# A carried state's products as four 64x64 products in the four quarters of TensorE

## The chip, the cores and the metric

The kernel runs on one core of one Trainium2 chip. The metric is the device time of one execution in microseconds; the time before is the median of three runs. All data is fp32.

## The reference, cut to what matters

A state-space layer (Mamba2 SSD) is followed by a sum of four gated two-layer networks. The layer works through a sequence in chunks. In each chunk it adds what the tokens of the chunk give one another (`y_intra`) to what the state carried over from earlier chunks gives (`y_inter`), and then renews the state:

```python
batch, n_heads, seq, head_dim, d_state = (4, 8, 768, 32, 16)
...
y_intra = np.einsum('bhij,bhjd->bhid', M, xc)
decay_to_i = np.exp(cum)
y_inter = np.einsum('bhin,bhnd->bhid', Cc, state) * decay_to_i[:, :, :, None]
y[:, :, sl] = y_intra + y_inter
...
state = decay_full[:, :, None, None] * state + np.sum(Bx, axis=2)
...
# second block: x is y with heads and head_dim joined, (3072, 256); E = 4, F = 1024
for e in range(E):
    h = np.maximum(x @ w1[e], 0.0)
    out += p[:, e:e + 1] * (h @ w2[e])
```

The change concerns `y_inter`, the product of `Cc` (16 state entries for each of 8 heads) with the state.

## The kernel before

The kernel cuts each of the 4 sequences into 6 chunks of 128 tokens: 24 chunks. Four chunks, one of each sequence, form a block of 512 tokens (`CPB = 4`, `NBLK = 6`); chunk `c` belongs to block `k = c // 4` and to sequence `i = c % 4`. The first block has no state yet, so 20 chunks have a product with it. The networks' products are done by Strassen's scheme (seven products of halves in place of eight) and fill most of TensorE's time; `fmul` is the first layer, `smul` the second.

The 8 heads lie as 4 groups `q` of 32 partitions, each with two heads `t`. A state product works on all 128 partitions: `lhsT` is `M`, the state, spread so that only the four 32x32 blocks on the diagonal are not zero, and `rhs` is `cts`, 2 x 128 = 256 columns.

```python
def load_tokens(c):
    xb = load.tile([P, W], FP32, tag="xb", name="xb", bufs=4)
    nc.sync.dma_start(out=xb, in_=xbc[real(c)])
    ...
def load_heads(c):
    ah = st[c]["ah"] = load.tile([HN, P], FP32, tag="ah", name="ah", bufs=4)
    nc.sync.dma_start(out=ah, in_=ac_d[real(c)].unsqueeze(1).to_broadcast([NH, N, P]))
...
# decay_part(c, 2): the decay of the state to each token, on the rows of C
    nc.vector.tensor_tensor_scan(out=dec, data0=s["ah"], data1=zeros, initial=1.0, ...)
    nc.gpsimd.tensor_mul(cts, s["ctm"], dec.unsqueeze(1).to_broadcast([HN, NT, P]))
...
def scores(cs, homes):                      # C times B, four row tiles of 32
    ...
    for j, c in enumerate(cs):
        for q in range(NQ):
            k = slice(32 * q, 32 * q + 32)
            nc.tensor.matmul(                                          # line 376
                out=s["g"][q]..., lhsT=s["xb"][k, OBT:OBT + P], rhs=s["ctm"][k]...,
                start=(j == 0), stop=True, tile_position=(32 * q, 0), ...)
...
def outputs(cs):                            # cs: two chunks
    for c in cs:
        ys[c] = y = ps_att.tile([P, NT, P + N], FP32, tag="att", name="y")
        if k > 0:
            nc.tensor.matmul(                                          # line 398
                out=y[:, :, 0:P], lhsT=state[i][1].rearrange("p q d -> p (q d)"),
                rhs=st[c]["cts"], start=True, stop=False, skip_group_check=True)
    for c in cs:
        for t in range(NT):
            for q in range(NQ):
                nc.tensor.matmul(                                      # line 408
                    out=y[32 * q:32 * q + 32, t, 0:w], lhsT=s["xb"][:, h * D:h * D + D],
                    rhs=s["MT"][:, NT * q + t, 0:w], tile_position=(0, 32 * q), ...)
    for c in cs:
        nc.scalar.copy(out=yT[k][:, :, i * P:i * P + P], in_=y[:, :, 0:P])   # line 417
        if k < NBLK - 1:
            s["A"] = att.tile([P, NT, N], FP32, tag="A", name="A", bufs=4)
            nc.scalar.copy(out=s["A"], in_=y[:, :, P:])                # line 420

def carry(c):                               # the new state S, and M for the next chunk
    nc.vector.transpose(S, s["A"]...)
    ...
    nc.vector.tensor_mul(M, S.unsqueeze(1).to_broadcast([HN, NQ, D]), qmask)
    state[c % CPB] = S, M
```

In the main loop, a step `n` is one part of the weights of a network (two steps for each network and block). Twice in a block of eight steps, two chunks of the next block are prepared: `scores` and `masked` at the end of one step, `outputs` within the next:

```python
    fmul(n, 6); snap(n, 6)                  # snap: ScalarE copies the bank X out
    smul(n - 1, 3)
    if done:
        outputs(done)                       # two chunks
        states.extend(done)
    fmul(n, 5); fmul(n, 7); snap(n, 7)
    total(n, 7, "22")                       # VectorE: z = Y + snap
    smul(n - 1, 7); smul(n - 1, 5)
    ...
```

Line 465 is `fmul`, line 550 `smul`, line 472 `snap`, line 477 `total` (tile `z`).

Of the kernel before, what the change touches and what calls it, by code (L numbers as in the profile page):

```python
# [12 lines left out]
P = 128  # L13
NQ, NT = 4, 2
# [3 lines left out]
def kernel(  # L18
# [38 lines left out]
    nc = tc.nc  # L57
# [3 lines left out]
    NH = NQ * NT  # L61
# [3 lines left out]
    CPB = BLK // P  # L65
    NBLK = NCH // CPB
    T = NCH * P
    OB, OBT, OCT = DM, DM + HN, DM + 2 * HN
    N = HN // NH
# [7 lines left out]
    def real(c):  # L77

        return c % CPB * NBLK + c // CPB
# [15 lines left out]
    ac_d = tc.dram_tile([NCH, NH, P], FP32, name="ac_d")  # L95
# [6 lines left out]
    st = {}  # L102
    SPREAD = 3

    def load_tokens(c):
        xb = load.tile([P, W], FP32, tag="xb", name="xb", bufs=4)
        nc.sync.dma_start(out=xb, in_=xbc[real(c)])
        st.setdefault(c, {})["xb"] = xb

    def load_decays(c):  # L110
# [5 lines left out]
    def load_heads(c):  # L116

        ah = st[c]["ah"] = load.tile([HN, P], FP32, tag="ah", name="ah", bufs=4)
        nc.sync.dma_start(out=ah, in_=ac_d[real(c)].unsqueeze(1).to_broadcast([NH, N, P]))

    def load_chunk(c):
        load_tokens(c)
        load_decays(c)
        load_heads(c)
# [66 lines left out]
    for queue, c in ((nc.sync, slice(0, 1)), (nc.scalar, slice(1, SPREAD))):  # L191
        queue.dma_start(
            out=a_q.rearrange("(q r) c t s -> q r c (t s)", q=NQ)[:, 0, c],
            in_=a.rearrange("(i k) (q t) s -> k q i (t s)", k=NBLK, t=NT)[0][:, c])
    warm = const.tile([P, 1], FP32, name="warm")
    nc.scalar.mul(warm, ones[:, 0:1], ones[:, 0:1])
    load_tokens(0)
    nc.sync.dma_start(
        out=a_sb, in_=a.rearrange("c h s -> (c h) s").rearrange("(p r) s -> p r s", r=2))
    load_tokens(1)  # L200
    load_w1(0)
    load_tokens(2)
# [161 lines left out]
    def scores(cs, homes):  # L364

        for c in cs:
            st[c]["g"] = []
        for pool, tag in homes:
            g = pool.tile([P, len(cs), NT, P], FP32, tag=tag, name="g")
            for j, c in enumerate(cs):  # L370
                st[c]["g"].append(g[:, j])
        for j, c in enumerate(cs):
            s = st[c]
            for q in range(NQ):
                k = slice(32 * q, 32 * q + 32)
                nc.tensor.matmul(  # L376
                    out=s["g"][q].rearrange("p t s -> p (t s)"), lhsT=s["xb"][k, OBT:OBT + P],
                    rhs=s["ctm"][k].rearrange("p t s -> p (t s)"),
                    start=(j == 0), stop=True, tile_position=(32 * q, 0),
                    skip_group_check=True)  # L380

    def masked(cs, qs):
        for q in qs:
            h = slice(NT * q, NT * q + NT)
            for c in cs:
                s = st[c]
                nc.vector.tensor_mul(s["MT"][:, h, 0:P], s["g"][q], s["LT"][:, h])  # L387

    state = {}

    def outputs(cs):

        ys = {}
        for c in cs:
            k, i = divmod(c, CPB)
            ys[c] = y = ps_att.tile([P, NT, P + N], FP32, tag="att", name="y")
            if k > 0:
                nc.tensor.matmul(  # L398
                    out=y[:, :, 0:P], lhsT=state[i][1].rearrange("p q d -> p (q d)"),
                    rhs=st[c]["cts"], start=True, stop=False, skip_group_check=True)  # L400
        for c in cs:
            s, y = st[c], ys[c]
            k, i = divmod(c, CPB)
            w = P + N if k < NBLK - 1 else P
            for t in range(NT):
                for q in range(NQ):
                    h = NQ * t + q
                    nc.tensor.matmul(  # L408
                        out=y[32 * q:32 * q + 32, t, 0:w], lhsT=s["xb"][:, h * D:h * D + D],
                        rhs=s["MT"][:, NT * q + t, 0:w], start=(k == 0 and t == 0), stop=True,  # L410
                        tile_position=(0, 32 * q), skip_group_check=True)
        for c in cs:
            s, y = st[c], ys[c]
            k, i = divmod(c, CPB)
            if i == 0:
                yT[k] = ffn.tile([P, NT, BLK], FP32, tag="yT", name="yT")
            nc.scalar.copy(out=yT[k][:, :, i * P:i * P + P], in_=y[:, :, 0:P])
            if k < NBLK - 1:
                s["A"] = att.tile([P, NT, N], FP32, tag="A", name="A", bufs=4)
                nc.scalar.copy(out=s["A"], in_=y[:, :, P:])  # L420

    def carry(c):
        s = st.pop(c)
# [234 lines left out]
    homes = ((ps_s, "acc0"), (ps_s, "acc1"), (ps_att, "att"), (ps_att, "att"))  # L658
# [12 lines left out]
    turn(1, 3)  # L671
    masks(0)
    scores([0], homes)
    decays(0)
    masks(1)
    spread(1)
    store_decays()
    masks(2)
    masked([0], range(NQ))
    outputs([0])  # L680
    scores([1], banks)
    decays(1)
    turn_gates(ps_att, "att")
    spread(2, (0,))
    spread_gate(ps_att, "att")
    masked([1], range(NQ))
    outputs([1])
    spread(2, (1,))
    sum_w1(0, 0)
# [5 lines left out]
    decays(2)  # L695
    plain_first(0, 1, (0,))
    scores([2], homes)
    plain_first(0, 1, (1,))
    masks(3)
# [4 lines left out]
    load_w2(3)  # L704
    gated(0, "11", "X")
    masked([2], range(NQ))
    outputs([2])

    scores([3], ((ps_s, "acc0"), (ps_s, "acc1"), (ps_s, "acc2"), (ps_att, "att")))
# [36 lines left out]
    for n in range(PLAIN, NS):  # L746
        k, r = divmod(n, SPB)
# [63 lines left out]
        for c in done:  # L811
            if c + CPB < NCH:
                load_tokens(c + CPB)
                load_heads(c + CPB)
# [74 lines left out]
```

## Time and profile before

| | |
|---|---|
| time, median of 3 runs | 646.47 us (646.44 to 647.34) |
| span of the profiled run | 643.5 us |
| TensorE busy | 636.3 us (99%) |
| VectorE busy | 483.9 us (75%) |
| ScalarE busy | 115.5 us (18%) |
| GpSimd busy | 108.3 us (17%) |
| granted TensorE clock | 0.998 of full speed |
| state products (line 398) | 40 records for 20 chunks, first at 69.4 us, last at 525.8 us |

PE is TensorE's matmul, PEld its loading of weights, DVE VectorE, ACT ScalarE, POOL GpSimd, SP the engine that issues most loads. A line of the groups gives the line of the kernel, the engine, the operation, the tile written and the tiles read, the shape (for a matmul rows * columns of the array, then the output), the count, and after the bar the busy time in all, the mean duration of one in ns and the idle time before them. Matmuls are pipelined, so a duration overlaps the next one; the distance between starts tells what one costs. An fp32 matmul leaves two records.

### The profile page before, as it was taken

What the parts mean: (1) busy time and instruction counts of PE and PEld (TensorE: products, weight loads), DVE (VectorE), ACT (ScalarE), POOL (GpSimd) and SP (SyncE); (2) the same over time, 40 slices, a digit from 0 to 9 for tenths busy, and PEclk for the clock granted to TensorE, in tenths of its full rate; (3) what the DMA queues carried; (4) which work ended last, traced back from release to release, by engine and by line L of the source; (5) the groups of instructions that cost most, each with busy time, mean ns of one, the idle gap of its engine ahead of it and who ended that gap; (6) DMA issues with size and microseconds to landing.
All of it is one profiled execution on the core that took longest, in us unless ns stands there. A gap on an engine that the chain in (4) does not pass through costs nothing.

```text
span 643.5 us, 9107 instructions
## 1 busy us (share of the span) xinstructions
PE 636.3 (99%) x3367; PEld 544.7 (85%) x3367; DVE 483.9 (75%) x809; ACT 115.5 (18%) x247; POOL 108.3 (17%) x157
## 2 busy tenths in 40 slices
PE   8999999999999999999999999999999999999997
PEld 5788878888888888888888888888888888888886
DVE  7869998788777688778688778768877667756555
ACT  3011121212111121112121211122121211111110
POOL 4788565020001002100002000000100000100000
PEclk9999999999999999999999999999999999999999
DMA  7987982855576391668284557548265744256000
GB/s 228 329 293 249 335 324 91 317 182 163 173 210 240 101 356 52 236 182 250 84 294 148 170 185 218 213 147 311 83 214 151 261 152 130 63 169 220 1 0 34
DMA packets 95648, 121.61 MB, mean 189 GB/s; under 512 B 28520, under 2 KB 77556, under 8 KB 95604
## 3 DMA queue, kind: packets, MB, share of 16 engines
q1 hardware_dynamic: 92776, 111.20, 52.8%
q0 software_dynamic: 2304, 9.44, 3.8%
q8 instruction: 27, 0.44, 0.3%
q10 hardware_dynamic: 524, 0.39, 0.2%
q14 instruction: 17, 0.14, 0.1%
HBM read 108.16 MB, written 12.83 MB: 188 GB/s over the span
## 4 chain that ended last, share of the span: by engine, by line
PE 96%; DVE 1%; DMA 1%; SPq 0%; ACT 0%; issue 0%; POOL 0%; ACTq 0%; DVEq 0%; POOLq 0%
PE acc L550 43%; PE X L465 24%; PE Y L465 19%; PE acc L531 2%; PE y L408 2%; PE g L376 2%; PE y L398 1%; PE X L514 1%; PE Y L514 1%; DMA xb<-in_xbc_dram 1%; DVE hT L494 0%; DVE h L487 0%; DVE z L477 0%; DVE LT L348 0%; SPq L134 0%
## 5 line engine op out<-in xcount | busy, mean ns | idle before, releaser
L477 DVE TENSOR_TENSOR z<-Y,snap 128x512 f32<-128x512 f32 x138 | 94.5, 685 | 127.5 <-ACT snap L472 76.4
L550 PE MATMUL acc<-hT,wt 128*128 128x256 f32 x736 | 181.3, 379 | 0.0
L472 ACT COPY snap<-X 128x512 f32<-128x512 f32 x138 | 80.8, 586 | 468.4 <-PE X L465 392.3
L550 PEld LDWEIGHTS acc<-hT,wt 128*128 128x128 f32 x736 | 140.0, 190 | 18.8
L550 PE MATMUL acc<-h,wt 128*128 128x256 f32 x552 | 142.6, 381 | 0.0
L465 PE MATMUL X<-yS,wt 128*128 128x256 f32 x552 | 141.8, 379 | 0.0
L550 PEld LDWEIGHTS acc<-h,wt 128*128 128x128 f32 x552 | 104.2, 190 | 16.9 <-issue 3.0
L465 PEld LDWEIGHTS X<-yS,wt 128*128 128x128 f32 x552 | 105.0, 190 | 14.3 <-issue 0.3
L487 DVE SCALAR_TENSOR_TENSOR h<-z,gate 128x512 f32<-128x512 f32 x138 | 100.1, 725 | 3.5 <-PE acc L531 0.4
L465 PE MATMUL Y<-yT,wt 128*128 128x256 f32 x368 | 94.7, 380 | 1.2 <-DVE z L477 1.2
L465 PEld LDWEIGHTS Y<-yT,wt 128*128 128x128 f32 x368 | 68.8, 190 | 12.3 <-DVE z L477 1.9
L494 DVE TENSOR_TENSOR hT<-h,hT 128x512 f32<-128x512 f32 x92 | 65.2, 709 | 1.8
L494 DVE TENSOR_TENSOR hT<-h,h 128x512 f32<-128x512 f32 x92 | 65.6, 754 | 1.1
L348 DVE TENSOR_TENSOR_SCAN LT<-ab,ident 128x512 f32<-128x512 f32 x42 | 52.1, 1242 | 0.0
L465 PE MATMUL Y<-yS,wt 128*128 128x256 f32 x184 | 48.3, 385 | 0.0
L465 PE MATMUL X<-yT,wt 128*128 128x256 f32 x184 | 47.3, 379 | 0.0
L353 POOL TENSOR_TENSOR MT<-xb,LT 128x128 f32<-128x128 f32 x20 | 8.5, 427 | 208.6 <-PE Y L465 100.3
L465 PEld LDWEIGHTS Y<-yS,wt 128*128 128x128 f32 x184 | 34.2, 190 | 6.4 <-issue 2.0
L465 PEld LDWEIGHTS X<-yT,wt 128*128 128x128 f32 x184 | 35.0, 190 | 4.7
L487 DVE SCALAR_TENSOR_TENSOR h<-X,gate 128x512 f32<-128x512 f32 x50 | 34.2, 685 | 5.9 <-PE X L465 3.6
L387 DVE TENSOR_TENSOR MT<-g,LT 128x256 f32<-128x256 f32 x96 | 33.0, 415 | 5.9 <-PE g L376 5.9
L334 POOL TENSOR_TENSOR cts<-ctm,dec 128x256 f32<-128x256 f32 x20 | 14.1, 726 | 133.9 <-DVE dec L331 133.9
(94 smaller groups left out, 329.0 us busy)
## 6 DMA issues: line engine op xcount, KB each, us to landing
wt<-in_w_dram SPq DMA_DIRECT2D x112, 256.0 KB, 6.5
wt<-w_d SPq DMA_DIRECT2D x40, 640.0 KB, 7.8
wt<-w_d SPq DMA_DIRECT2D x40, 512.0 KB, 7.4
ab<-acut_d SPq DMA_DIRECT2D x21, 512.0 KB, 8.4
xb<-in_xbc_dram SPq DMA_DIRECT2D x24, 320.0 KB, 3.4
gate<-p_d SPq DMA_DIRECT2D x23, 256.0 KB, 8.3
w_d<-wt POOLq DMA_DIRECT2D x8, 640.0 KB, 3.6
wt<-in_w_dram SPq DMA_DIRECT2D x40, 128.0 KB, 4.4
```

What stands on the lines that cost most here:

```text
L334: nc.gpsimd.tensor_mul(cts, s["ctm"], dec.unsqueeze(1).to_broadcast([HN, NT, P]))
L348: nc.vector.tensor_tensor_scan(out=LT[:, i * w:i * w + w], data0=s["a"][i], data1=ident.rearrange("p h s -> p (h s)")[:, :w], initial=0.0, ...
L376: nc.tensor.matmul(out=s["g"][q].rearrange("p t s -> p (t s)"), lhsT=s["xb"][k, OBT:OBT + P], rhs=s["ctm"][k].rearrange("p t s -> p (t s)" ...
L387: nc.vector.tensor_mul(s["MT"][:, h, 0:P], s["g"][q], s["LT"][:, h])
L408: nc.tensor.matmul(out=y[32 * q:32 * q + 32, t, 0:w], lhsT=s["xb"][:, h * D:h * D + D], rhs=s["MT"][:, NT * q + t, 0:w], start=(k == 0 and ...
L465: nc.tensor.matmul(out=f[bank][:, j], lhsT=wt1[n][:, w, j * P:j * P + P], rhs=rhs, start=(i in (1, 2, 5) and j == 0), stop=(j == JJ - 1), ...
L472: nc.scalar.copy(out=s, in_=first[n]["X"])
L477: nc.vector.tensor_add(z, first[n]["Y"], first[n][i])
L487: nc.vector.scalar_tensor_tensor(out=h, in0=first[n][src], scalar=0.0, in1=g.unsqueeze(1).to_broadcast([P, JJ, HB]), op0=ALU.max, op1=ALU. ...
L494: nc.vector.tensor_sub(h[o], h[x], h[y])
L514: nc.tensor.matmul(out=f[bank][:, j], lhsT=wt1[n][:, w, j * P:j * P + P], rhs=yT[k][:, i, cols], start=(i == 0 and j == 0), stop=(i == 1), ...
L550: nc.tensor.matmul(out=acc[k, u][:, half], lhsT=w2_op(n, w)[:, j], rhs=rhs[:, j], start=(begins and j == 0), stop=(n % SPB == SPB - 1 and ...
```

## The change

The block-diagonal `M` has two 64x64 quarters on its diagonal and two that are all zero. The change does only the two diagonal quarters of each chunk, as 64x64 products that each take one quarter of the array. In each pair of chunks, the second (`c` odd) has its two halves of partitions changed over: its `B`, `C` and decays are loaded with the halves exchanged, its state lies exchanged, and its products read the lower 64 partitions and write the upper 64, and the other way round. So the four products of a pair take the four quarters of the array, and can run side by side. The tokens `x` and the outputs `y` keep their places.

For that, odd chunks load `xb` in three parts and `ah` in two, the bank of a group of scores is looked up exchanged, and `A`, from which the state is renewed, is copied in two halves that change places.

```diff
+    HALF = P // 2
+    def turned_round(c):
+        return c >= CPB and c % 2 == 1
 
     def load_tokens(c):
         xb = load.tile([P, W], FP32, tag="xb", name="xb", bufs=4)
-        nc.sync.dma_start(out=xb, in_=xbc[real(c)])
+        src = xbc[real(c)]
+        if turned_round(c):
+            nc.sync.dma_start(out=xb[:, :OBT], in_=src[:, :OBT])
+            nc.sync.dma_start(out=xb[:HALF, OBT:], in_=src[HALF:, OBT:])
+            nc.sync.dma_start(out=xb[HALF:, OBT:], in_=src[:HALF, OBT:])
+        else:
+            nc.sync.dma_start(out=xb, in_=src)
 ...
-        nc.sync.dma_start(out=ah, in_=ac_d[real(c)].unsqueeze(1).to_broadcast([NH, N, P]))
+        src = ac_d[real(c)].unsqueeze(1).to_broadcast([NH, N, P])
+        if turned_round(c):
+            nc.sync.dma_start(out=ah[:HALF], in_=src[NH // 2:])
+            nc.sync.dma_start(out=ah[HALF:], in_=src[:NH // 2])
+        else:
+            nc.sync.dma_start(out=ah, in_=src)
 ...   (scores, masked: the bank of row tile r is that of group r ^ 2 in a turned chunk)
             if k > 0:
-                nc.tensor.matmul(
-                    out=y[:, :, 0:P], lhsT=state[i][1].rearrange("p q d -> p (q d)"),
-                    rhs=st[c]["cts"], start=True, stop=False, skip_group_check=True)
+                for a_ in range(2):
+                    rows = slice(HALF * a_, HALF * a_ + HALF)
+                    to = HALF * (1 - a_ if turned_round(c) else a_)
+                    nc.tensor.matmul(
+                        out=y[to:to + HALF, :, 0:P],
+                        lhsT=state[i][1].rearrange("p q d -> p (q d)")[rows, rows],
+                        rhs=st[c]["cts"][rows], start=True, stop=False,
+                        tile_position=(HALF * a_, to), skip_group_check=True)
 ...
                 s["A"] = att.tile([P, NT, N], FP32, tag="A", name="A", bufs=4)
-                nc.scalar.copy(out=s["A"], in_=y[:, :, P:])
+                if i % 2:
+                    nc.scalar.copy(out=s["A"][:HALF], in_=y[HALF:, :, P:])
+                    nc.scalar.copy(out=s["A"][HALF:], in_=y[:HALF, :, P:])
+                else:
+                    nc.scalar.copy(out=s["A"], in_=y[:, :, P:])
```

More of the change, by code (lines that the diff above doesn't have):

```diff
@@ L366, in scores, with masked @@
         for c in cs:
-            st[c]["g"] = []
-        for pool, tag in homes:
+            st[c]["g"] = {}
+        for r, (pool, tag) in enumerate(homes):
             g = pool.tile([P, len(cs), NT, P], FP32, tag=tag, name="g")
             for j, c in enumerate(cs):
-                st[c]["g"].append(g[:, j])
+                st[c]["g"][r ^ 2 * turned_round(c)] = g[:, j]
         for j, c in enumerate(cs):
             s = st[c]
-            for q in range(NQ):
-                k = slice(32 * q, 32 * q + 32)
+            for r in range(NQ):
+                k = slice(32 * r, 32 * r + 32)
+                g = s["g"][r ^ 2 * turned_round(c)]
                 nc.tensor.matmul(
-                    out=s["g"][q].rearrange("p t s -> p (t s)"), lhsT=s["xb"][k, OBT:OBT + P],
+                    out=g.rearrange("p t s -> p (t s)"), lhsT=s["xb"][k, OBT:OBT + P],
                     rhs=s["ctm"][k].rearrange("p t s -> p (t s)"),
-                    start=(j == 0), stop=True, tile_position=(32 * q, 0),
+                    start=(j == 0), stop=True, tile_position=(32 * r, 0),
                     skip_group_check=True)
-    def masked(cs, qs):
-        for q in qs:
-            h = slice(NT * q, NT * q + NT)
+    def masked(cs, rs):
+        for r in rs:
             for c in cs:
+                q = r ^ 2 * turned_round(c)
+                h = slice(NT * q, NT * q + NT)
                 s = st[c]
```

## The prediction

> **What bounds the kernel now.** I read the page from the top: the busy shares first, then the chain that ended last, then the stretches, and only then single lines. The shares and the chain:
>
> ```profile
> PE 636.3 (99%) x3367; PEld 544.7 (85%) x3367; DVE 483.9 (75%) x809; ACT 115.5 (18%) x247; POOL 108.3 (17%) x157
> ...
> PE 96%; DVE 1%; DMA 1%; SPq 0%; ACT 0%; issue 0%; POOL 0%; ACTq 0%; DVEq 0%; POOLq 0%
> ```
>
> TensorE (PE) is busy 99% of a span of 643.5 us and is 96% of the chain. A busy PE is not a PE at its peak, so I asked for its own waits. The list is almost empty; after the start-up one entry remains, 1.2 us long, for the sum `z` of VectorE (DVE):
>
> ```profile
> PE Y L465 <- DVE z L477: 1.2, 1, 1.2
> PE t L665 <- DVE ones L188: 1.1, 1, 1.1
> PE gp L283 <- ACT p_sb L274: 0.6, 1, 0.6
> ```
>
> So from about 90 us on, one time slot of TensorE taken away is one slot off the end. The change touches line 398. The groups by form give its weight, and that of the two tiled products around it:
>
> ```profile
> L376 PE MATMUL g<-ctm,xb 32*128 32x256 f32 x192 | 14.4, 405 | 0.0
> L408 PE MATMUL y<-MT,xb 128*32 128x144 f32 x320 | 12.3, 290 | 0.0
> L398 PE MATMUL y<-cts,M 128*128 128x256 f32 x40 | 10.3, 379 | 0.0
> L420 ACT COPY A<-y 128x32 f32<-128x32 f32 x20 | 3.8, 192 | 0.0
> ```
>
> Line 398 has 40 records for 20 chunks: an fp32 product leaves two records. A record lasts 379 ns, but they are pipelined, so I take the distance between starts from the timeline (start, duration, line, tile, number of records). Around the first such pair:
>
> ```profile
> 68.75 1.03 PE L550 MATMUL acc<-h,wt 128*128 128x256 f32 x4
> 69.61 1.03 PE L398 MATMUL y<-cts,M 128*128 128x256 f32 x4
> 70.56 1.19 PE L408 MATMUL y<-MT,xb 128*32 128x144 f32 x32
> 71.68 1.13 PE L465 MATMUL Y<-yS,wt 128*128 128x256 f32 x4
> 72.65 1.03 PE L465 MATMUL X<-yS,wt 128*128 128x256 f32 x4
> ```
>
> Four full records take 69.61 - 68.75 = 0.86 us, that is 0.216 us each. The state products of two chunks are four records and hold TensorE 70.56 - 69.61 = 0.95 us: 0.86 of streaming and 0.09 for going over to the column-tiled products. The other tiled group, four row tiles of 32, shows what several tiles do:
>
> ```profile
> 61.43 1.03 PE L550 MATMUL acc<-hT,wt 128*128 128x256 f32 x4
> 62.38 1.15 PE L376 MATMUL g<-ctm,xb 32*128 32x256 f32 x16
> 63.46 1.13 PE L550 MATMUL acc<-h,wt 128*128 128x256 f32 x4
> 64.43 0.38 PE L550 MATMUL acc<-hT,wt 128*128 128x256 f32 x1
> ```
>
> Sixteen records of 256 columns in 63.46 - 62.38 = 1.08 us, where sixteen full ones would take 3.45. So they run four at a time (4 x 0.216 = 0.86), and 0.22 us is the price of going in and out of the tiled form. Entry costs another 0.09 (62.38 - 61.43 less 0.86), and the first full products after it come 0.11 late (64.43 - 63.46 less 0.86).
>
> **What the Trainium skill says.** "TensorEngine Tiling (Array Packing)", section Tiling Modes: 64x64 is one of the forms and gives four independent tiles, but changing the form drains the engine. The trace agrees with the drain: it is the 0.09 us at each border. The same page, section Restrictions and Gotchas, says that different row tiles must not be at one PSUM bank at the same time. Here the two quarters that write the same partitions belong to two chunks, whose `y` lie in two banks; the two quarters that write one bank write different partitions. Line 376 is the first case (four row tiles, four banks) and line 408 the second (four column tiles, one bank), and in the trace both run four wide. "TensorE: Matmul & The Clock Gate", section Part 3: Packing small matmuls, states that row and column tiles compose; no product in this trace is tiled both ways at once, so this is the one thing I take on trust.
>
> **The change part by part.** *TensorE.* Per pair of chunks, two 128x128 products (four records) become four 64x64 products (eight records) of the same 256 columns. The weights `M` are block-diagonal at 32 rows, so two of the four quarters of each full product multiplied nothing but zeros. A chunk's two diagonal quarters alone would leave two quarters idle; the odd chunk, with halves changed over, uses the other two. In the program order the two records of one quarter follow each other, as the two of a row tile do in line 376, and there the engine still runs four tiles side by side. So I expect two steps of four records.
>
> The new time from the first state product to the first `y<-MT` product, against 0.95 now: entry from the full form 0.09. First step: 0.216 plus the weight load that cannot be hidden across the border. That extra was 0.10 in line 376 (first group at 62.38, second at 62.70 in the trace, with a weight load of 185 ns) and 0.02 in line 408 (70.56 to 70.71 for 144 columns, 121 ns by the same rate, with a load of 109 ns); a 64-column load should lie between, and I put 0.05. Second step 0.216. Going over to line 408: 0.09, and 0.02 because the last of the four starts that much after the first. Sum 0.09 + 0.27 + 0.22 + 0.11 = 0.69 us. Saved per pair 0.95 - 0.69 = 0.26; if the first load costs the whole 0.10, 0.21. There are 20 chunks with a state, 10 pairs: 2.1 to 2.6 us. Lines 408, 376 and everything else on TensorE keep number and shape.
>
> *ScalarE (ACT).* The odd chunks' `A` is copied in two halves: 10 more copies. A copy of 32 elements is all fixed cost (192 ns), so about 1.9 us more in all, 0.19 in each pair. ScalarE is busy 18%. The copies come after the `yT` copies, and the next `snap` waits for the second of two products of four records each, some 1.7 us later, so nothing on the path moves.
>
> *DMA.* For 10 chunks one `xb` load becomes three and one `ah` load two: 30 more issues on SyncE. An issue of `xb` took 0.36 us at the median and one of `ah` 0.63, so three more cost the queue about 1 us per odd chunk. Rows are 1536 and 1024 bytes instead of 2560: 1280 more packets on 95648, no more bytes. The loads behind it in the queue are weights, asked for two steps ahead (a step is about 12 us) into five buffers. That margin swallows 1 us.
>
> *DVE and GpSimd* keep their instructions, order and shapes; only some scans wait for two landings in place of one.
>
> *The one wait.* At 88.74 TensorE waits 1.2 us for DVE, just after the first pair at 69.6. Would the wait eat the first saving? DVE's chain up to it began at 81.55 on a product `Y`, after 0.61 us of idle time:
>
> ```profile
> 81.55 0.69 DVE L477 TENSOR_TENSOR z<-Y,snap 128x512 f32<-128x512 f32 x1 [0.61 <-PE Y L465]
> ```
>
> TensorE 0.26 earlier makes DVE start 0.26 earlier there, within that idle time. So the pair counts. Later the stretches of 64 us show TensorE busy 64.00 of 64.00 with DVE at 44 to 50, so DVE has room to follow.
>
> Sum: -2.4 (middle of 2.1 to 2.6), +0.1 for anything lost to queueing at the start: -2.3. With a first load cheaper than I put it, -2.8. I take -2.5: 646.47 - 2.5 = 644.0 us, 0.4%.
>
> **Rivals.** *The four quarters run only two wide.* Then four steps of 0.216 and the same borders: 0.09 + 0.27 + 3 x 0.216 + 0.11 = 1.12 against 0.95, a loss of 0.17 per pair, 648.2 us. For it: row and column tiling together occurs nowhere in this trace, and each bank gets writes from two row tiles. Against it: each half of the combination runs four wide. *They run one after the other*, eight steps: 1.98 against 0.95, +10 us, 656.8. Against it: the hardware passes over the second record of a tile to start the next tile's first, seen at line 376. *TensorE's gain turns into waits for DVE or for loads*: nothing comes off, 646.5 plus at most 1 us at the start, where the DMA engines are 83% busy over the first 64 us and GpSimd prepares weights. Against it: weights and sums are ahead of their use, and the list of waits has no DMA on TensorE. *More gain than reckoned*: the borders could cost less between two tiled forms than between a tiled and the full form; then 0.1 more per pair, 643.0.
>
> **Range and chances.** Measured runs of the kernel before spread over 0.9 us, and the terms I am unsure of (load extra 0.02 to 0.10, border 0 to 0.1) are worth about 1 us over ten pairs. I put 643.0 to 645.4, which leaves about one chance in ten for narrower concurrency. 2% would be 12.9 us; only serial quarters come near it, so "within 2%" is almost sure.
>
> **What would show it.** Line 398's successor has 80 records of 64x64, starts in two bunches of four per pair, and the distance from its first start to the first `y<-MT` record falls from 0.95 to about 0.6 (entry counted before it, 0.95 instead of 0.86 from the product ahead). PE's busy time falls by 2 to 3 us and its list of waits stays as short. `A` copies number 30. What would make it wrong: four or eight evenly spaced starts per pair; a new wait of TensorE for a weight load before 100 us; the stop at 88.7 longer by the time saved.

## The result, and the profile after

The changed kernel took 641.79 us at the median (641.22 to 641.98, 4 runs) against 646.46 us for the kernel before (645.01 to 647.34, 4 runs: the three from ahead of the prediction and one more, of 645.01 us): a ratio of 0.9928 (95% interval 0.9909 to 0.9948). That is 4.7 us less, and below the predicted range of 643.0 to 645.4. Two later comparisons of the two kernels put the difference lower, at 3.0 and 3.6 us; they are told with the experiments.

The busy shares and the chain that ended last, from the page of the kernel after:

```profile
PE 633.0 (99%) x3407; PEld 538.3 (84%) x3407; DVE 483.7 (76%) x809; ACT 118.4 (19%) x257; POOL 108.2 (17%) x157
...
PE 97%; DVE 1%; DMA 1%; issue 0%; ACT 0%; POOL 0%; SPq 0%; DVEq 0%; ACTq 0%; POOLq 0%
```

Nothing took TensorE's place. It has 40 records more (3407) and is busy 3.3 us less; VectorE stays at 484 us, ScalarE has ten copies and 2.9 us more. TensorE's own waits are as short as before, and the wait for `z` has neither grown nor gone (it now lies at 87.5 us):

```profile
PE Y L494 <- DVE z L506: 1.2, 1, 1.2
PE t L694 <- DVE ones L206: 1.1, 1, 1.1
PE g L395 <- ACT ctm L380: 0.2, 1, 0.2
```

The changed group and its neighbours, by form (count, then busy us and mean ns). Line 421 is line 398 of before, 433 is 408, 395 is 376, and 446 and 447 are the two halves of the copy of `A`:

```profile
L395 PE MATMUL g<-ctm,xb 32*128 32x256 f32 x192 | 14.3, 404 | 0.2 <-ACT ctm L380 0.2
L433 PE MATMUL y<-MT,xb 128*32 128x144 f32 x320 | 12.7, 290 | 0.0
L421 PE MATMUL y<-cts,M 64*64 64x256 f32 x80 | 6.6, 402 | 0.0
L421 PEld LDWEIGHTS y<-cts,M 64*64 64x64 f32 x80 | 2.1, 131 | 3.3 <-issue 2.7 <-POOL wt L182 0.3 <-DVE z L506 0.3
L446 ACT COPY A<-y 64x32 f32<-64x32 f32 x10 | 1.8, 182 | 0.1
L447 ACT COPY A<-y 64x32 f32<-64x32 f32 x10 | 1.8, 177 | 0.1
```

Twice the records of the state product, 80 for 40, with 6.6 us of busy time instead of 10.3. The first pair in TensorE's timeline (start, duration, line, tile, records):

```profile
67.79 1.03 PE L579 MATMUL acc<-h,wt 128*128 128x256 f32 x4
68.75 0.66 PE L421 MATMUL y<-cts,M 64*64 64x256 f32 x8
69.34 1.19 PE L433 MATMUL y<-MT,xb 128*32 128x144 f32 x32
70.46 1.13 PE L494 MATMUL Y<-yS,wt 128*128 128x256 f32 x4
```

From the product ahead to the first `y<-MT` it is 69.34 - 67.79 = 1.55 us; before it was 70.56 - 68.75 = 1.81. From the first state product it is 69.34 - 68.75 = 0.59 us, where 0.95 was to fall to about 0.6. The same timeline cut at 68.74 to 68.78 us shows the four quarters starting together:

```profile
68.75 0.45 PE L421 MATMUL y<-cts,M 64*64 64x256 f32 x4
```

In ns, from the starts of the records: the border into the tiled form takes 309 from the last full record, the second four start 267 after the first four, and the next form starts 326 after that. That is 902 ns against 1172 before, 270 less. All ten pairs give 901 or 902, and 1171 to 1173 before.

So the mechanism is as predicted. Ten pairs are worth 2.7 us, and the first comparison showed 4.7: the experiments look for the rest.

### The profile page after: what moved, and what is told of

It is laid out like the page before. It is cut to its first block, busy times and chain, and to the rows that moved or that the text cites. A ratio compares the mean times of both kernels' runs of the same rounds, so it can differ in the third digit from the quotient of the medians.

```text
span 639.4 us, 9224 instructions
## 1 busy us (share of the span) xinstructions
PE 633.0 (99%) x3407; PEld 538.3 (84%) x3407; DVE 483.7 (76%) x809; ACT 118.4 (19%) x257; POOL 108.2 (17%) x157
## 4 chain that ended last, share of the span: by engine, by line
PE 97%; DVE 1%; DMA 1%; issue 0%; ACT 0%; POOL 0%; SPq 0%; DVEq 0%; ACTq 0%; POOLq 0%
PE acc L579 43%; PE X L494 25%; PE Y L494 19%; PE acc L560 2%; PE y L433 2%; PE g L395 2%; PE X L543 1%; PE Y L543 1%; PE y L421 1%; PE a L332 1%; DMA xb<-in_xbc_dram 1%; DVE hT L523 0%; DVE h L516 0%; DVE z L506 0%; DVE LT L366 0%
```

## The experiments

Matching TensorE's records of the two first traces one to one shows at which places the changed kernel gains: 0.95 us before the 14th microsecond, 0.27 at each of the ten pairs, nothing between them, and 0.37 after the last product. 0.95 + 2.71 + 0.37 = 4.03 us, the whole difference of the spans (643.48 and 639.45). Up to 13 us no engine has another instruction than before: ScalarE's first copy of `A` in two halves comes at 13.4 us, the first split load at 25.7. So **theory A** is that the 0.95 is chance in the arrival of the first loads. **Theory B** is that the change itself shortens start and end, by its split loads or copies. The first four kernels ran on one chip beside 51 runs of before (median 645.08 us, 644.11 to 648.35).

**Both kernels once more, unchanged.**

> The kernel before, unchanged, once more, to see how much its start varies. Theory A (the 0.95 us by which the changed kernel was ahead at 60 us is chance in the arrival of the first loads): the start of the third group of scores, 62.38 us in the first trace of before and 61.43 in the trace of after, falls somewhere between 61.2 and 63, and the time goes with it. Theory B (the change shortens the start): 62.3 to 62.5 again.

> The changed kernel, unchanged, once more. Theory A (chance at the start): its third group of scores starts anywhere from 61.2 to 63 us, and the ratio against before comes out nearer to 0.9958 (ten pairs of 0.27 us, 2.7 us) than to 0.9928. Theory B (the change itself shortens the start by 1 us): it starts at 61.3 to 61.5 again and the ratio stays near 0.993. Both: 10 gains of 0.27 us at the state products.

Measured: before again 644.89 us, ratio 0.9991 (0.9978 to 1.0004). After again 642.06 us, ratio 0.9940 (0.9918 to 0.9961). The two medians alone give 0.9953, nearer to theory A's 0.9958, but the ratio itself is nearer to the 0.9928 of theory B, and its interval holds both: the times don't decide, the starts in the traces do. The third group of scores, that of chunks 4 and 5, started at 62.02 us in before (62.38 the first time) and at 62.66 in after (61.43 the first time): the changed kernel was ahead at 60 us in one trace and behind in the other. The two traces of after:

```profile
61.43 1.15 PE L395 MATMUL g<-ctm,xb 32*128 32x256 f32 x16
```

```profile
62.66 1.15 PE L395 MATMUL g<-ctm,xb 32*128 32x256 f32 x16
```

ScalarE's timeline shows what moves it. First trace of before, then the two of after; L362 and L380 are the masking of C (`ctm`), here of the third chunk:

```profile
10.90 0.69 ACT L362 ACTIVATE ctm<-xb,tmask 128x128 f32<-128x128 f32 x2 [3.21 <-DMA xb<-in_xbc_dram]
11.50 0.35 ACT L417 COPY yT<-y 128x256 f32<-128x256 f32 x1
```

```profile
9.73 0.69 ACT L380 ACTIVATE ctm<-xb,tmask 128x128 f32<-128x128 f32 x2 [1.87 <-DMA xb<-in_xbc_dram]
10.34 0.35 ACT L442 COPY yT<-y 128x256 f32<-128x256 f32 x1
```

```profile
11.18 0.69 ACT L380 ACTIVATE ctm<-xb,tmask 128x128 f32<-128x128 f32 x2 [3.12 <-DMA xb<-in_xbc_dram]
11.78 0.35 ACT L442 COPY yT<-y 128x256 f32<-128x256 f32 x1
```

ScalarE stands still for the third token load, ahead of the copies of the first outputs in its order. The load came 1.45 us apart in two runs of one kernel, and the start of the scores follows it (10.90 to 62.38, 10.54 to 62.02, 11.18 to 62.66: 51.48 us each time; 9.73 to 61.43, 51.70, where something else begins to bind). So the whole 0.95 is within what one kernel's start varies by, as theory A has it; whether a smaller part of it is the change's stays open (see below). The medians differ by 3.0 us here, what the pairs and the end give, 2.7 + 0.37.

**The change without its small products.** It leaves out the 64x64 products and keeps all the rest.

```diff
-                for a_ in range(2):
-                    ... 64x64 products of the two quarters ...
+                nc.tensor.matmul(
+                    out=y[:, :, 0:P], lhsT=state[i][1].rearrange("p q d -> p (q d)"),
+                    rhs=st[c]["cts"], start=True, stop=False, skip_group_check=True)
...
-        nc.vector.tensor_mul(M, S.unsqueeze(1).to_broadcast([HN, NQ, D]), qmask)
+        turn_ = 2 * (c % 2)      # qmask two blocks wider, so that M's columns change over too
+        nc.vector.tensor_mul(
+            M, S.unsqueeze(1).to_broadcast([HN, NQ, D]), qmask[:, turn_:turn_ + NQ])
```

> The change without its 64x64 products: loads split and halves changed over, A copied in halves, M spread with its columns changed over, but each state product one full 128x128 product again. Theory A (all the systematic gain is at the state products): the time of before within 0.5 us, 646 to 647. Theory B (split loads or copies shorten something else): 644 to 645.3. A cost of the loads would show as 647 or more.

Measured: 644.56 us, ratio 0.9990 (0.9981 to 0.9999). Not the 646 of theory A, because before itself was now at 645.1; against that it is 0.5 us lower. Its timeline at the first pair has the old form and the old distance, 69.83 - 68.01 = 1.82 us:

```profile
68.01 1.03 PE L579 MATMUL acc<-h,wt 128*128 128x256 f32 x4
68.88 1.03 PE L421 MATMUL y<-cts,M 128*128 128x256 f32 x4
69.83 1.19 PE L431 MATMUL y<-MT,xb 128*32 128x144 f32 x32
```

So the loads and copies cost nothing and shorten nothing in the middle of the kernel (575.64 us from the third scores to the last `acc` product, against 575.65 and 575.64 in before). But the end was 0.37 us shorter here too, as in both traces of after, and not in the two of before. For the end, theory B holds: it goes with the loads.

**Two quarters only, nothing turned round.**

```diff
-                nc.tensor.matmul(
-                    out=y[:, :, 0:P], lhsT=state[i][1].rearrange("p q d -> p (q d)"),
-                    rhs=st[c]["cts"], start=True, stop=False, skip_group_check=True)
+                for a_ in range(2):
+                    rows = slice(P // 2 * a_, P // 2 * a_ + P // 2)
+                    nc.tensor.matmul(
+                        out=y[rows, :, 0:P],
+                        lhsT=state[i][1].rearrange("p q d -> p (q d)")[rows, rows],
+                        rhs=st[c]["cts"][rows], start=True, stop=False,
+                        tile_position=(P // 2 * a_, P // 2 * a_), skip_group_check=True)
```

> The kernel before with each state product as its two diagonal 64x64 quarters, no chunk turned round, loads and copies as before. If records of different quarters run side by side and those of one quarter one after the other, a pair takes four steps in two quarters: entry 0.31 us from the product ahead, first step 0.27, two of 0.216, 0.32 to the next form, 1.33 us against 1.17 before, so 1.6 us longer in all, 648.1. If the chunks' halves did not have to be in four different quarters to run four wide (the rival), it is as fast as the changed kernel, 0.90 us per pair.

Measured: 646.71 us, ratio 1.0023 (1.0014 to 1.0032), 1.6 us above the 645.08 of before, as reckoned; its trace gives 1.5 (1.32 us for 1.17 at each pair). The first pair:

```profile
68.73 1.03 PE L554 MATMUL acc<-h,wt 128*128 128x256 f32 x4
69.68 1.08 PE L400 MATMUL y<-cts,M 64*64 64x256 f32 x8
70.69 1.19 PE L412 MATMUL y<-MT,xb 128*32 128x144 f32 x32
```

The eight records now take 70.69 - 69.68 = 1.01 us, four steps of two: they start 309 and 315 ns after the last full record, then at 575 and 582, 791 and 798, 1007 and 1014. The same small products without the change of halves lose; it is the four different quarters that make them run four wide.

**Where the end comes from.** The records of SyncE's closing instructions, in us after the last `acc` product started: in before it passes the first semaphore at 2.20, stands until 3.96 at the second and until 4.19 at the third, and then passes six more at 0.06 each, to 4.55. In after it passes five more at 0.06 each up to 2.51, stands at 3.44, 3.96, and until 4.19 at the last. The waiting order is fixed; the three last stores signal whichever semaphores are next in turn, and the change has 30 issues more. Two kernels shift the turn alone, one in each direction:

```diff
 # kernel before
+        if c in (12, 14, 16):
+            for part in (slice(0, DM), slice(DM, OBT), slice(OBT, W)):
+                nc.sync.dma_start(out=xb[:, part], in_=xbc[real(c)][:, part])
+        else:
             nc.sync.dma_start(out=xb, in_=xbc[real(c)])
```

> The kernel before with three of its later token loads (chunks 12, 14, 16) each in three parts: six issues more, nothing else. Theory (the end is 0.37 us shorter in the changed kernel only because the number of loads shifts which semaphores the last stores signal, and SyncE waits for the semaphores in a fixed order): the time from the start of the last acc product to the end falls from 5.44 to 5.07 us, and the median is 0.2 to 0.5 us below before. Rival (turned data, or the split loads lying near each other, do something else): 5.44 us and no difference.

```diff
 # kernel after
+        elif c == 12:
+            nc.sync.dma_start(out=xb[:, :OBT], in_=src[:, :OBT])
+            nc.sync.dma_start(out=xb[:, OBT:], in_=src[:, OBT:])
```

> The changed kernel with one more issue (the token load of chunk 12 in two parts). Theory of the order of semaphores: the last of the three stores now signals the semaphore that SyncE waits for first, so the end is 5.4 us again and the time 0.3 to 0.4 us above the changed kernel's, about 642.4 against 642.06. Rival: the end stays at 5.08 us.

Measured, beside 27 runs of before at 645.14 us: before with split loads 644.63 us, ratio 0.9995 (0.9986 to 1.0004), end 5.08 us. After with one more load 642.23 us, ratio 0.9956 (0.9943 to 0.9970), end 5.52 us. Both ends moved as the theory said, one trace each; a third of a microsecond lies within the scatter of the medians, so the traces carry this and not the times. In the traces the last store's issue on ScalarE and the span give it. Kernel before, and before with split loads:

```profile
core 0 of [0], span 643.5 us
639.80 0.36 ACTq L632 DMA_DIRECT2D out_dram<-rows  x1
```

```profile
core 0 of [0], span 643.3 us
640.04 0.36 ACTq L636 DMA_DIRECT2D out_dram<-rows  x1
```

3.7 us from that issue to the end in the first, 3.3 in the second, with the same instructions on the way. Kernel after, and after with one more load, 3.3 and 3.7:

```profile
core 0 of [0], span 639.4 us
636.14 0.36 ACTq L661 DMA_DIRECT2D out_dram<-rows  x1
```

```profile
core 0 of [0], span 640.4 us
636.66 0.36 ACTq L664 DMA_DIRECT2D out_dram<-rows  x1
```

**Can the chance at the start be taken out?** `masks(2)` is moved behind `spread_gate`, so that ScalarE doesn't stand still for the third token load so early.

```diff
     store_decays()
-    masks(2)
     masked([0], range(NQ))
...
     spread_gate(ps_att, "att")
+    masks(2)
     masked([1], range(NQ))
```

> The kernel before with masks(2), the first use of the third token load, moved behind spread_gate(2): ScalarE then need not stand still for that load ahead of the copies of the first outputs. Theory (the start varies because ScalarE waits in order for the third token load, which arrives at 9.7 to 11.2 us): the third group of scores starts at 61.4 us or earlier, and stays there, and the median falls by 0.5 to 1 us to about 644.2, with a narrower spread. Rival (the chance sits elsewhere): the start still varies over 1 us and the median stays at 645.

> The changed kernel with the same move of masks(2). Theory: third group of scores at 61.4 us or earlier, time 641.0 to 641.5, ratio to before about 0.994 less 0.001; and the distance to the kernel before with the same move is 3.1 us (2.7 at the state products and 0.37 at the end). Rival: no difference from the changed kernel, 642.

Measured: before with it 644.51 us (ratio 0.9993, 0.9983 to 1.0003), after with it 641.23 us (0.9938, 0.9926 to 0.9950). The two with the move are 3.3 us apart, where 3.1 was expected. The wait is gone from ScalarE ahead of the first copies, but the third group of scores started at 61.59 and 61.88 us, not at 61.4 or earlier. Once more, beside the changed kernel:

> The changed kernel a third time, beside the one with masks(2) moved, on one chip. From the parts found so far (ten pairs of 0.271 us, 0.37 us at the end) it should be 3.1 us below before, ratio 0.9952, give or take the chance at the start; 642.0 if before is at 645.1.

> The changed kernel with masks(2) behind spread_gate(2), a second time. If the move takes out the part of the chance that comes from the third token load, its median lies 0.3 to 0.8 us below the changed kernel's of this call; if the 641.23 us of the first run was chance, both medians are within 0.2 us.

Measured: after 641.59 us, ratio 0.9940 (0.9923 to 0.9958), 3.6 us below the 645.23 of before where 3.1 was expected; with the move 641.65 us, 0.9945 (0.9927 to 0.9962). The 641.23 was chance, and the move gains nothing that can be measured. Other loads at the start vary as well: the first scores, which come ahead of the moved work, started between 5.88 and 6.69 us over all traces.

The traces together, in us; "middle" is from the third group of scores to the start of the last `acc` product and holds all ten pairs:

| kernel | third scores | middle | end |
|---|---|---|---|
| before, two traces | 62.38, 62.02 | 575.65, 575.64 | 5.45, 5.44 |
| before, split loads | 62.63 | 575.64 | 5.08 |
| before, late masks | 61.59 | 575.64 | 5.44 |
| change, whole products | 61.65 | 575.64 | 5.07 |
| two quarters only | 62.37 | 577.12 | 5.45 |
| after, three traces | 61.43, 62.66, 61.72 | 572.93, 572.92, 572.93 | 5.08, 5.08, 5.08 |
| after, one more load | 61.97 | 572.92 | 5.52 |
| after, late masks, two traces | 61.88, 61.62 | 572.93, 572.93 | 5.07, 5.07 |

The middle repeats to 0.01 us: 2.72 us of the gain lie there, 0.37 at the end, and the start scatters over 1.2 us.

## Why the prediction was right or wrong

*The size per pair* was right: 0.26 us predicted, 0.27 measured, ten times. Entry 0.309 - 0.216 = 0.09 as put. The first step, guessed between two other forms as 0.27, was 0.267, with weight loads of 131 ns, between the 109 and 185 used for the guess. The border to the column-tiled form was the same 0.09 as from the full one, so the rival "the borders cost less" is out.

*Row and column tiling together*, the thing taken on trust from the skill's "TensorE: Matmul & The Clock Gate", section Part 3: Packing small matmuls, is borne out: four 64x64 records start within 20 ns. The rivals "two wide" and "one after the other" are out. The restriction on row tiles and banks that the prediction quotes did not bind as it is worded: the two quarters of one chunk are different row tiles and write one `y` bank, in different partitions, and they start 6 to 7 ns apart. Line 408, taken as the precedent, has a single row tile and is none.

*Off the path.* ScalarE's copies (2.9 us more in busy time, put at 1.9) and the split loads moved nothing in the middle: the kernel that has them without the small products keeps 575.64 us. The packets rose by 1600 and not by 1280; I left out 320 of 4 bytes. The three extra issues of an odd chunk were put at about 1 us of SyncE; the figures given for them make 2 x 0.36 + 0.63 = 1.35, and the trace shows 1.7. The wait for `z` stayed at 1.2 us, so the first pair's gain was kept, and with 0.27 us at all ten pairs the rival "the gain turns into waits" is out.

*What failed* is the step "Range and chances", and in it the base. I took 646.47 us, the median of three runs, for the place of the kernel before, and their spread of 0.9 us for all that it could be off by. 89 later runs in three comparisons have medians of 645.08, 645.14 and 645.23: the three lay 1.3 us above that, and only 7 of the 89 were as high as the lowest of the three. The changed kernel's four runs were nothing unusual (641.79 us, later 642.06 and 641.59). So the first difference of 4.7 us was too large by the base, and not by the early start in the trace of after. A sign was at hand: the execution of before that was profiled took 645.25 us. The same range laid around 645.1 is 641.6 to 644.0, with 641.79 near its lower end.

*Missing from the sum* was the end. I had +0.1 for queueing at the start, which did not show, and nothing for the end, which gave -0.37. With 2.71 for the pairs the gain is 3.1 us; the two later comparisons of the changed kernel give 645.08 - 642.06 = 3.0 and 645.23 - 641.59 = 3.6, and with one load more it is 645.14 - 642.23 = 2.9 for the kernel whose end is long again (2.7 from the parts). From 645.1 that would have been 642.0.

*Open* is the last half microsecond. The scores of the kernels with turned loads started on average some 0.4 us earlier than those of the others, in a handful of traces that scatter over 1.2. With the late masks it is the other way round (61.59 in before, 61.88 and 61.62 in after), and the third load, where the starts part, is waited for before any instruction differs; both speak for chance and do not settle it. Nor is it known why the first three runs of before were as high as they were.

## What to carry to other kernels

Block-diagonal products that leave quarters of the array multiplying zeros can be packed by letting a second, independent product use the other quarters, if its operands can be loaded with halves of partitions exchanged; the loads are the cheap part. Price it by steps and borders: each step of four records took what one full record takes, and each change of form took 0.09 us and a part of the first weight load, so that halving the tiles without filling all four quarters lost. A gain below 1% needs a base of more than three runs, and a look at the traces' start and end before the difference of two medians is put down to the change.

## What the runs showed that was not expected

The order in which this kernel's last stores signal their semaphores was worth 0.37 us: SyncE passes them in a fixed order at 0.06 us each, and loads added earlier in the program shift it, in either direction (six more: 5.44 to 5.08 us; one more: 5.08 to 5.52).

In the kernel each product is one instruction that leaves two records, yet four records of a pair started together and the other four 267 ns later; with only two quarters in use, the eight ran in four steps of two. The prediction has it that the hardware passes over a tile's second record; whether it does, or the compiled program already holds the records in that order, the traces do not tell.
